# Chunked attention and two MLPs on one core: later issue of raw weight loads, g fetched three steps ahead, other places for late k, q, v loads and for y's copies

## Chip, core and metric

One core of one Trainium2 chip runs the whole program. The metric is device time in microseconds (us) of one execution, the median of several. Engines are named as in the profile: PE (matmul), PEld (its weight load), DVE, ACT, POOL and SP. SP issues nearly all loads, POOL the stores to scratch tensors in DRAM.

## Reference

Attention runs inside chunks of 64 tokens, and its result goes through two MLPs:

```python
scores = scale * np.matmul(q_c, k_c.transpose(0, 1, 2, 4, 3))     # q, k, v: (4, 8, 576, 64), chunks of 64
attn = softmax(scores)
x = (attn @ v_c)  -> (2304 tokens, 512)
x = ((x @ w_a) * (x @ w_b)) @ w_out                               # d_ff 1536
h = x @ w_in                                                      # d_ff 2048
g = (a0 + a1*h + a2*h**2 + a3*h**3) / (1 + |b0|*|h| + |b1|*h**2 + 1e-6)
out = g @ w_out2
```

All inputs are read as pairs of 32-bit words where they are 64-bit numbers (the weights), and every product is made from a high and a low part of both factors: three matmuls for one.

## The kernel before

**The order of the program.** One core walks through five stages. (1) The head: attention of the first 768 tokens (units of 128 tokens, numbered `u`, 0 to 5), in an order written out by hand in two lists. `LOADS` is the order of the first loads on SP's queue; `FIRST` is the order of the work: `k0` transposes k of unit 0, `S` makes scores, `X` the exponential, `E` the softmax's division, `P` transposes the result, `V` multiplies with v, `L` makes the low part of x, `w` is one piece of a weight's conversion, and `d4` puts 4 matmuls on a constant tile with no use for their result on PE (`warm`). Units 0 to 2 are done in the head, 3 to 5 within the next stage. (2) `ab_half`: x times `w_a` and `w_b` for the first 768 tokens, with attention of the other tokens between. (3) `s_step`: the same products for the other tokens, in a scheme with seven products for eight. Both store g = a*b to DRAM, `g_d[i]` for the 12 blocks `i` of d_ff. (4) The y stage: 5 blocks of tokens `j` (256, then 512 each) by 12 blocks `i`, `y_part(j, i)`, which fetches g back from DRAM (`g_fetch`), splits it in high and low (`g_parts`, the cast on ACT at L650, the difference on DVE at L652), and adds into four PSUM tiles `acc[j][d]`. Those are copied out by `y_out` (ACT, L673) and stored by POOL. (5) `step2`: the second MLP.

**Weights.** A raw weight tile (512 KB, 64-bit) is loaded by `w_fetch` (L169), converted in four pieces (`w_piece`), and split into high and low. The pieces are spread through the program by `w_until`. Piece 0 reads the raw tile on ACT (L214) and DVE (L218), piece 2 reads it for the last time on ACT (L223). The first 24 tiles (`w_a`, `w_b` alternating, named w_a_0, w_b_1, w_a_2, ... by their number) have 4 raw buffers, the later ones 2. Loads of the tiles behind are issued in pieces 0 and 2 by `w_fetch_ahead`. Each waits on SP until the buffer's last reader, L223 of the tile 4 or 2 before, is done, and all that stands behind it on SP's queue waits too.

**Small buffers.** Fetched g, fetched y, converted tiles `w_x`, g to be stored and copies `ys` share six buffers (`p_io`, tag `io`). `g_hi` and `g_lo` have two each.

**Order between engines.** The schedule is manual: every engine runs its instructions in the order in which the code calls them. In the y stage a step `n` issues `g_fetch` of step n+2, then `g_parts` of step n+1, pieces of weights, then `y_part` of step n, and `evacuate(1)` takes one `y_out` from the list `evac`. In step2's first calls the list is emptied after the front of the second MLP. PSUM tile `ps_ab` "a" holds `acc[4][2]` in the last block and is then the tile of the third `h_part` (L247 to L249, h).

Of the kernel before, what the change touches and what calls it, by code (L numbers as in the profile page):

```python
# [20 lines left out]
def chunk_attention_two_mlps(  # L21
# [34 lines left out]
    nc = tc.nc  # L56
    P = 128
# [7 lines left out]
    KD = DM // P  # L65
    F1 = DFF1 // P
# [11 lines left out]


    FIRST = (  # L80
        "k0 d2 q0 k1 q1 S0 X0 d4 S1 X1 k2 E0 w w q2 E1 P0 S2 w w V0 d2 P1 X2 L0 w w V1 E2 w w L1 d2 P2 w w V2 L2 w"
    ).split()
    LOADS = "k0 q0 k1 q1 w v0 k2 q2 w v1 v2 w k3 q3 w k4 q4 v3 k5 q5 v4 v5".split()

    AHEAD = 4
    NWP = 12 - AHEAD
# [54 lines left out]
    order1 = [(n, i) for i in range(F1) for n in ("a", "b")]  # L141
# [41 lines left out]
    def w_fetch_ahead(n):  # L183
        while n_cv[0] < n_cv[2] and n_cv[0] < n + (AHEAD if n_cv[0] < len(order1) else 2):
            w_fetch()

    def w_hi(n):
        if n in f32s:
            key = order[n]
            wt[key] = w_tile(key, F32R)  # L190
            nc.scalar.copy(wt[key][0], f32s[n].bitcast(F32))

    def w_lo(n):
        if n in f32s:
            hi, lo = wt[order[n]]
            nc.vector.tensor_tensor(lo, f32s.pop(n).bitcast(F32), hi.bitcast(F32), ALU.subtract)

    def w_piece():


        n, piece = divmod(n_cv[1], 4)
        n_cv[1] += 1
        key = order[n]
        if piece == 0:
            w_fetch_ahead(n)
            t = raws.pop(key)

            terms[n] = (t, *w_tile(key, I32))
        t, c, z = terms[n]
        hw = t[:, :, 1]  # L210
        lw = t.rearrange("p f t -> p (f t)").bitcast(U16).rearrange("p (f t) -> p f t", t=4)[:, :, 1]
        zz = z.bitcast(F16).rearrange("p (f t) -> p f t", t=2)
        if piece == 0:
            nc.scalar.activation(zz[:, :, 1], hw.bitcast(F32), AF.Copy, scale=2.0 ** -112)  # L214
            if 8 <= n < len(order1) + len(ordero):
                nc.scalar.activation(c.bitcast(F32), hw.bitcast(F32), AF.Copy, scale=2.0 ** -112)
            else:
                nc.vector.tensor_scalar(c.bitcast(F32), hw.bitcast(F32), 2.0 ** -112, None, ALU.mult)  # L218
        elif piece == 1:
            w_hi(n - 1)  # L220
            nc.vector.tensor_scalar(c, c, 3, None, ALU.logical_shift_left)
        elif piece == 2:
            nc.scalar.activation(zz[:, :, 0].bitcast(U16), lw, AF.Copy, scale=2.0 ** -13)  # L223
            w_lo(n - 1)
            w_fetch_ahead(n + 1)
        else:
            del terms[n]
            x = f32s[n] = p_io.tile([P, DM], I32, name="w_x", tag="io")
            nc.vector.tensor_tensor(x, c, z, ALU.add)
            if key in w1_d:  # L230
                nc.gpsimd.dma_start(out=w1_d[key], in_=x.bitcast(F32))

    def w_until(tiles):

        while n_cv[1] < min(4 * tiles, 4 * n_cv[2]):
            w_piece()
# [14 lines left out]
    def cols(pair, k):  # L251
        return [t[:, k * P:(k + 1) * P] for t in pair]
# [43 lines left out]
    def a_load(u, *names):  # L296

        (b0, c0), (b1, c1) = divmod(2 * u, NCH), divmod(2 * u + 1, NCH)
        for nm, src in (("k", k), ("q", q), ("v", v)):
            if nm not in names or u >= NU:  # L300
                continue
            if u < 2 * UH:
                if ("raw", u) not in un:
                    un["raw", u] = p_X.tile([P, 3, H, D], F32, name="kqv", tag=f"X{NQ - 1}_{u + 1}")
                t = un["raw", u][:, "kqv".index(nm)]
            else:
                t = p_qk.tile([P, H, D], F32, name=nm, tag=nm, bufs=2 if nm == "v" else 1)
            if b0 == b1:
                parts = [(t, src[b0, :, c0 * CH:(c0 + 2) * CH, :])]
            else:  # L310
                parts = [
                    (t[c * CH:(c + 1) * CH], src[bb, :, cc * CH:(cc + 1) * CH, :])
                    for c, (bb, cc) in enumerate(((b0, c0), (b1, c1)))
                ]
            for dst, s in parts:
                nc.sync.dma_start(out=dst, in_=s.rearrange("h s d -> s h d"))  # L316
            raw[nm, u] = t
# [154 lines left out]
    ca_t = const.tile([P, 4], F32, name="ca_t")  # L472
    cb_t = const.tile([P, 2], F32, name="cb_t")
# [156 lines left out]
    acc = {}  # L630
    evac = []
# [9 lines left out]
    def g_fetch(j, i):  # L641
        t = p_io.tile([P, SIZES[j]], F32, name="g_raw", tag="io")
        nc.sync.dma_start(out=t, in_=g_d[i][:, START[j]:START[j] + SIZES[j]])
        raw["g", j, i] = t
# [9 lines left out]
    def y_part(j, i):  # L654

        if i == 0:
            places = [(ps_acc, "acc")] * 2
            places += [(ps_at, "at")] * 2 if j % 2 else [(ps_ab, "a"), (ps_ab, "b")]
            acc[j] = [pool.tile([P, SIZES[j]], F32, name="acc", tag=tag) for pool, tag in places]
        w, (gh, gl) = wt["o", i], g1.pop((j, i))  # L660
        for d in range(KD):
            wh, wl = cols(w, d)
            nc.tensor.matmul(acc[j][d], wh, gh, start=i == 0, stop=False)  # L663
            nc.tensor.matmul(acc[j][d], wl, gh, start=False, stop=False)  # L664
        for d in range(KD):
            wh, wl = cols(w, d)
            nc.tensor.matmul(acc[j][d], wh, gl, start=False, stop=i == F1 - 1)  # L667
            if i == F1 - 1:
                evac.append(lambda d=d: y_out(j, d))

    def y_out(j, d):
        ys = p_io.tile([P, SIZES[j]], F32, name="ys", tag="io")
        nc.scalar.copy(ys, acc[j][d])  # L673
        nc.gpsimd.dma_start(out=y_d[:, d, START[j]:START[j] + SIZES[j]], in_=ys)

    def evacuate(n):
        for _ in range(min(n, len(evac))):
            evac.pop(0)()
# [122 lines left out]

    for item in LOADS:
        if item == "w":
            w_fetch()
        else:
            a_load(int(item[1]), item[0])
    nc.sync.dma_start(out=ca_t, in_=ca.unsqueeze(0).to_broadcast([P, 4]))
    nc.sync.dma_start(out=cb_t, in_=cb.unsqueeze(0).to_broadcast([P, 2]))
    nc.vector.memset(nlsh[:, 0:1], (1.0 + 1e-6) * 2.0 ** -LSH)
    nc.vector.memset(nlsh[:, 1:2], -LSH * math.log(2.0))  # L810

    for item in FIRST:
        if item == "w":
            w_piece()
            continue
        if item[0] == "d":
            warm(int(item[1:]))
            continue
        what, u = item[:-1], int(item[-1])
        if what in "kq":  # L820
            a_transpose(u, what)
        else:
            {"S": a_scores, "X": a_exp, "E": a_soft, "P": a_ptrans, "V": a_pv, "L": lambda u: un.pop(("lo", u))()}[
                what
            ](u)
    for u in (2 * UH, 2 * UH + 1):
        a_load(u, "k", "q", "v") if u == 2 * UH else a_load(u, "v")

# [35 lines left out]
    def half():  # L864


        n = n_half[0]
        n_half[0] += 1
        w_until(min(11 + 2 * n, 32) / 4 if n < 17 else (n + 18) / 4)
        if n_cv[1] == 32 or n_cv[1] == 4 * len(order1):  # L870
            w_flush()
        tick(0.5)
# [50 lines left out]
    w_until(n_cv[2])  # L923
    g_parts(0, 0)()
    g_fetch(0, 2)
    third, last = prev
    third()
    w_flush()
# [12 lines left out]
    places = [(j, i) for j in range(NB) for i in range(F1)]  # L941
# [2 lines left out]
    done = n_cv[1]  # L944
    a_ring = None
    for n, (j, i) in enumerate(places):
        if 0 < n < len(places) - 2:
            g_fetch(*places[n + 2])
        due = done + (4 * len(order2) * spent[n] // spent[-1] if n < len(spent) else 4 * len(order2))
        due -= n_cv[1]  # L950
        low = lambda: None
        if n + 1 < len(places):
            low = g_parts(*places[n + 1])
        if due:
            w_piece()
        low()
        for _ in range(due - 1):
            w_piece()
        if n:
            y_part(j, i)  # L960
        evacuate(1)
        if j == NB - 1:
            if 2 <= i < 2 + KD:
                y_split(0, i - 2)
            if 1 <= i < 1 + KD:
                y_fetch(0, i - 1)
            if i >= F1 - EARLY:
# [38 lines left out]
```

## Time and profile before

| | us |
|---|---|
| median of 3 runs (947.08 to 947.53) | 947.42 |
| the profiled execution's own time | 946.14 |
| span shown by its profile | 944.4 |
| PE busy within the span | 901.9 |

The profile is of one execution, whose time is 1.28 us below the median. The span is the stretch from the first to the last instruction, and the 1.74 us to the execution's time lie around it. An engine's busy time is of instructions alone; waits and the issuing of loads are not in it. PE is busy for 95% of the span, so what PE does not use is 42.5 us in all. PEclk is the share of full clock that PE was granted: 1.00 is 2.4 GHz and 0.50 is 1.2 GHz.

### The profile page before, as it was taken

What the parts mean: (1) busy time and instruction counts of PE and PEld (TensorE: products, weight loads), DVE (VectorE), ACT (ScalarE), POOL (GpSimd) and SP (SyncE); (2) the same over time, 40 slices, a digit from 0 to 9 for tenths busy, and PEclk for the clock granted to TensorE, in tenths of its full rate; (3) what the DMA queues carried; (4) which work ended last, traced back from release to release, by engine and by line L of the source; (5) the groups of instructions that cost most, each with busy time, mean ns of one, the idle gap of its engine ahead of it and who ended that gap; (6) DMA issues with size and microseconds to landing.
All of it is one profiled execution on the core that took longest, in us unless ns stands there. A gap on an engine that the chain in (4) does not pass through costs nothing.

```text
span 944.4 us, 14722 instructions
## 1 busy us (share of the span) xinstructions
PE 901.9 (95%) x5516; PEld 793.1 (84%) x5516; DVE 725.4 (77%) x1328; ACT 607.0 (64%) x1098; POOL 64.3 (7%) x122
## 2 busy tenths in 40 slices
PE   6879999999999999799998989999999999999998
PEld 5769998989999998676766889888888888888997
DVE  5657878588788875566656589899888988998886
ACT  5647887455555453466656478786777777776775
POOL 0111111111111111000000000000000000000000
PEclk9879999999999999999999999999999999999999
DMA  9957896333443413566776320020002002000100
GB/s 233 249 170 213 245 236 184 119 120 129 140 140 122 144 65 129 190 207 228 230 234 224 130 67 1 1 78 0 1 1 89 1 0 79 1 1 1 45 1 33
DMA packets 107335, 105.82 MB, mean 112 GB/s; under 512 B 61440, under 2 KB 84480, under 8 KB 107264
## 3 DMA queue, kind: packets, MB, share of 16 engines
q1 hardware_dynamic: 99264, 79.71, 29.1%
q0 software_dynamic: 8000, 25.17, 7.3%
q8 instruction: 43, 0.70, 0.3%
q14 instruction: 28, 0.23, 0.1%
HBM read 74.98 MB, written 29.88 MB: 111 GB/s over the span
## 4 chain that ended last, share of the span: by engine, by line
PE 52%; issue 24%; DMA 7%; ACT 5%; DVE 4%; SPq 4%; POOL 3%; POOLq 0%; ACTq 0%; DVEq 0%
PE h L247 7%; PE h L249 7%; PE acc L248 7%; PE h L248 7%; PE acc L247 7%; PE acc L249 7%; DMA g_raw<-g_d 6%; POOL g_d L487 3%; SPq L316 2%; PE ab L247 2%; PE ab L249 2%; PE ab L248 2%; ACT g_hi L650 1%; SPq L169 1%; PE acc L663 1%
## 5 line engine op out<-in xcount | busy, mean ns | idle before, releaser
L247 PE MATMUL h<-y,w_i 128*128 128x512 f32 (+1 forms) x320 | 118.7, 371 | 3.0 <-ACT ys L673 3.0
L249 PE MATMUL h<-y,w_i 128*128 128x512 f32 (+1 forms) x320 | 118.5, 370 | 0.0
L248 PE MATMUL h<-y,w_i 128*128 128x512 f32 (+1 forms) x320 | 118.3, 370 | 0.0
L724 ACT ACTIVATE a_ring<-h 128x512 f32<-128x512 f32 (+1 forms) x80 | 44.3, 554 | 99.6 <-PE h L249 99.5
L663 PE MATMUL acc<-g_hi,w_o 128*128 128x512 f32 (+1 forms) x240 | 90.2, 383 | 14.1 <-ACT g_hi L650 12.4
L573 ACT COPY s<-y 128x384 f32<-128x384 f32 x72 | 34.4, 479 | 84.6 <-PE y L249 83.0
L664 PE MATMUL acc<-g_hi,w_o 128*128 128x512 f32 (+1 forms) x240 | 87.9, 373 | 0.0
L727 DVE SCALAR_TENSOR_TENSOR u<-u,cb_t,a_ring 128x512 f32<-128x512 f32 (+1 forms) x80 | 55.7, 696 | 35.3 <-ACT u L725 34.4
L652 DVE TENSOR_TENSOR g_lo<-g_raw,g_hi 128x512 fp32r<-128x512 f32 (+1 forms) x60 | 38.1, 636 | 54.4 <-ACT g_hi L650 51.2
L248 PE MATMUL acc<-w_o,g_hi 128*128 128x512 f32 x191 | 75.3, 394 | 0.0
L650 ACT CAST g_hi<-g_raw 128x512 fp32r<-128x512 f32 (+1 forms) x60 | 34.1, 570 | 63.4 <-DMA g_raw<-g_d 49.0
L247 PE MATMUL acc<-w_o,g_hi 128*128 128x512 f32 x191 | 74.9, 392 | 0.0
L249 PE MATMUL acc<-w_o,g_lo 128*128 128x512 f32 x191 | 74.2, 389 | 0.0
L663 PEld LDWEIGHTS acc<-g_hi,w_o 128*128 128x128 f32 x240 | 45.3, 189 | 30.5 <-ACT g_hi L650 20.9
L247 PEld LDWEIGHTS h<-y,w_i 128*128 128x128 f32 x320 | 60.5, 189 | 12.2 <-ACT ys L673 3.3
L248 PEld LDWEIGHTS h<-y,w_i 128*128 128x128 f32 x320 | 60.6, 190 | 8.7
L249 PEld LDWEIGHTS h<-y,w_i 128*128 128x128 f32 x320 | 60.5, 189 | 7.5
L667 PE MATMUL acc<-g_lo,w_o 128*128 128x512 f32 (+1 forms) x240 | 60.9, 376 | 0.6 <-DVE g_lo L652 0.6
L726 ACT ACTIVATE t<-h,ca_t 128x512 f32<-128x512 f32 (+1 forms) x80 | 59.1, 738 | 0.0
L729 DVE SCALAR_TENSOR_TENSOR t<-t,ca_t,h 128x512 f32<-128x512 f32 (+1 forms) x80 | 55.6, 695 | 2.8
L737 DVE SCALAR_TENSOR_TENSOR u<-u,r 128x512 f32<-128x512 f32 (+1 forms) x80 | 50.5, 631 | 9.1 <-ACT r L736 9.1
L736 ACT ACTIVATE r<-r,nlsh 128x512 f32<-128x512 f32 (+1 forms) x80 | 54.6, 682 | 2.6
(196 smaller groups left out, 2444.0 us busy)
## 6 DMA issues: line engine op xcount, KB each, us to landing
w_raw<-in_moe_w_out_dram SPq DMA_DIRECT2D x28, 512.0 KB, 3.7
g_d<-g POOLq DMA_DIRECT2D x72, 192.0 KB, 2.4
g_raw<-g_d SPq DMA_DIRECT2D x48, 256.0 KB, 4.2
w_raw<-in_moe_w_in_dram SPq DMA_DIRECT2D x16, 512.0 KB, 3.9
w_raw<-in_moe_w_a_dram SPq DMA_DIRECT2D x12, 512.0 KB, 5.3
w_raw<-in_moe_w_b_dram SPq DMA_DIRECT2D x12, 512.0 KB, 5.3
out_dram<-o SPq DMA_DIRECT2D x18, 256.0 KB, 2.3
y_d<-ys POOLq DMA_DIRECT2D x16, 256.0 KB, 4.5
```

What stands on the lines that cost most here:

```text
L247: nc.tensor.matmul(ps, wh, xh, start=first, stop=False, **kw)
L248: nc.tensor.matmul(ps, wh, xl, start=False, stop=False, **kw)
L249: nc.tensor.matmul(ps, wl, xh, start=False, stop=last, **kw)
L663: nc.tensor.matmul(acc[j][d], wh, gh, start=i == 0, stop=False)
L664: nc.tensor.matmul(acc[j][d], wl, gh, start=False, stop=False)
L667: nc.tensor.matmul(acc[j][d], wh, gl, start=False, stop=i == F1 - 1)
L724: nc.scalar.activation(ah, ps, AF.Abs)
L726: nc.scalar.activation(t, ps, AF.Identity, scale=ca_t[:, 3:4], bias=ca_t[:, 2:3])
L727: nc.vector.scalar_tensor_tensor(u, u, cb_t[:, 0:1], ah, ALU.add, ALU.mult)
L729: nc.vector.scalar_tensor_tensor(t, t, ca_t[:, 1:2], ps, ALU.add, ALU.mult)
L736: nc.scalar.activation(r, r, AF.Exp, scale=-1.0, bias=nlsh[:, 1:2])
L737: nc.vector.scalar_tensor_tensor(u, u, 1.0 + 1e-6, r, ALU.add, ALU.mult)
```

## The change

Eight edits, none of which changes what is computed. The head gets 12 more `warm` matmuls. Loads of k5, q5, v3, v4 and v5 are taken from `LOADS` and stand in `FIRST` (the `+` items), so that three raw weight tiles come ahead of them; the two small constants `ca_t`, `cb_t` are loaded after the head's list. In the `ab_half` stage `w_until` is called for two pieces more. From the 24th tile on, `w_fetch_ahead` moves from piece 2 to piece 3. `g_fetch` runs three steps ahead. The first `y_part` puts three low matmuls ahead of the fourth d. And `y_out` takes d in the order 2, 3, 0, 1.

```diff
     FIRST = (
-        "... E1 P0 S2 w w V0 d2 P1 X2 L0 w w V1 E2 w w L1 d2 P2 w w V2 L2 w"
+        "... E1 P0 S2 w +k5 +q5 w V0 d2 P1 X2 L0 w w V1 d4 E2 w +v3 +v4 +v5 w "
+        "L1 d2 P2 d4 w w V2 d4 L2 w"
     ).split()
-    LOADS = "k0 q0 k1 q1 w v0 k2 q2 w v1 v2 w k3 q3 w k4 q4 v3 k5 q5 v4 v5".split()
+    LOADS = "k0 q0 k1 q1 w v0 k2 q2 w v1 v2 w k3 q3 w k4 q4".split()
...
         elif piece == 2:
             nc.scalar.activation(zz[:, :, 0].bitcast(U16), lw, AF.Copy, scale=2.0 ** -13)
             w_lo(n - 1)
+            if n < len(order1):
+                w_fetch_ahead(n + 1)
+        else:
             w_fetch_ahead(n + 1)
-        else:
             del terms[n]
...
-        for d in range(KD):
-            wh, wl = cols(w, d)
-            nc.tensor.matmul(acc[j][d], wh, gl, start=False, stop=i == F1 - 1)
-            if i == F1 - 1:
-                evac.append(lambda d=d: y_out(j, d))
+            if (j, i) == (0, 0) and d == KD - 2:
+                for x in range(d + 1):
+                    nc.tensor.matmul(acc[j][x], cols(w, x)[0], gl, start=False, stop=False)
+        for d in range(KD - 1 if (j, i) == (0, 0) else 0, KD):
+            nc.tensor.matmul(acc[j][d], cols(w, d)[0], gl, start=False, stop=last)
+        if last:
+            evac.extend(lambda d=d: y_out(j, d) for d in (2, 3, 0, 1))
...
-        w_until(min(11 + 2 * n, 32) / 4 if n < 17 else (n + 18) / 4)
+        w_until(min(13 + 2 * n, 32) / 4 if n < 17 else (n + 18) / 4)
...
     g_fetch(0, 2)
+    g_fetch(0, 3)
...
-        if 0 < n < len(places) - 2:
-            g_fetch(*places[n + 2])
+        if 0 < n < len(places) - 3:
+            g_fetch(*places[n + 3])
```

**SP's queue in the head.** These are the loads that follow v1 and v2. `kqv` is a unit's k, q or v, `w_raw` a raw weight tile, in the order w_a_2, w_b_3, then w_a_4, w_b_5, w_a_6. Before:

```order
L316 DMA kqv<-in_q_dram 64x8x64 x2
L316 DMA kqv<-in_v_dram 128x8x64
L316 DMA kqv<-in_k_dram 128x8x64
L316 DMA kqv<-in_q_dram 128x8x64
L316 DMA kqv<-in_v_dram 64x8x64 x2
L316 DMA kqv<-in_v_dram 128x8x64
L807 DMA ca_t<-in_moe_a_dram 128x4
L808 DMA cb_t<-in_moe_b_dram 128x2
L169 DMA w_raw<-in_moe_w_a_dram 128x4x256
L169 DMA w_raw<-in_moe_w_b_dram 128x4x256
L169 DMA w_raw<-in_moe_w_a_dram 128x4x256
```

And of the change:

```order
L319 DMA kqv<-in_q_dram 64x8x64 x2
L170 DMA w_raw<-in_moe_w_a_dram 128x4x256
L319 DMA kqv<-in_k_dram 128x8x64
L319 DMA kqv<-in_q_dram 128x8x64
L170 DMA w_raw<-in_moe_w_b_dram 128x4x256
L319 DMA kqv<-in_v_dram 128x8x64
L319 DMA kqv<-in_v_dram 64x8x64 x2
L319 DMA kqv<-in_v_dram 128x8x64
L170 DMA w_raw<-in_moe_w_a_dram 128x4x256
L834 DMA ca_t<-in_moe_a_dram 128x4
L835 DMA cb_t<-in_moe_b_dram 128x2
```

w_a_4 moves ahead of k5 and q5, w_b_5 ahead of v3 to v5, and w_a_6 ahead of the constants. What stands behind these rows (k6 and q6, v6 and v7, then w_b_7) has the same loads ahead of it as before.

**SP's queue in the y stage's first block.** `g_raw` are fetches of g, `w_raw` the raw tiles of the second MLP's weights. Before:

```order
L169 DMA w_raw<-in_moe_w_in_dram 128x4x256
L169 DMA w_raw<-in_moe_w_out_dram 128x1024
L643 DMA g_raw<-g_d_82 128x256
L643 DMA g_raw<-g_d_83 128x256
L643 DMA g_raw<-g_d_84 128x256
L643 DMA g_raw<-g_d_85 128x256
L169 DMA w_raw<-in_moe_w_in_dram 128x4x256
L643 DMA g_raw<-g_d_86 128x256
L643 DMA g_raw<-g_d_87 128x256
L643 DMA g_raw<-g_d_88 128x256
```

And of the change:

```order
L646 DMA g_raw<-g_d_82 128x256
L170 DMA w_raw<-in_moe_w_in_dram 128x4x256
L170 DMA w_raw<-in_moe_w_out_dram 128x1024
L646 DMA g_raw<-g_d_83 128x256
L646 DMA g_raw<-g_d_84 128x256
L646 DMA g_raw<-g_d_85 128x256
L646 DMA g_raw<-g_d_86 128x256
L646 DMA g_raw<-g_d_87 128x256
L170 DMA w_raw<-in_moe_w_in_dram 128x4x256
L646 DMA g_raw<-g_d_88 128x256
```

The numbers 82 to 88 are the blocks i = 3 to 9. The fetches of i = 7 and i = 8 now stand ahead of the third raw tile, which in both programs waits on SP for a piece on ACT. The last four fetches of the stage stand together at its end, as before.

**ACT at the end of the y stage.** `acc_5805` to `acc_5808` are before's four tiles `acc[4][0]` to `acc[4][3]`; in the change they are `acc_5822` to `acc_5825`. `h` is the second MLP's first product in its first and second step. Before:

```order
L673 COPY ys_6122<-acc_5805 128x512
L735 ACTIVATE r_6138<-u_6102,nlsh_144 128x384
L736 ACTIVATE r_6138<-r_6138,nlsh_144 128x384
L724 ACTIVATE a_ring_6088<-h_6125 128x384
L725 ACTIVATE u_6102<-h_6125,cb_t_143 128x384
L726 ACTIVATE t_6103<-h_6125,ca_t_142 128x384
L116 CAST g_hi_6150<-t_6103 128x384
L673 COPY ys_6154<-acc_5806 128x512
L673 COPY ys_6157<-acc_5807 128x512
L673 COPY ys_6160<-acc_5808 128x512
```

And of the change:

```order
L680 COPY ys_6137<-acc_5824 128x512
L742 ACTIVATE r_6153<-u_6117,nlsh_144 128x384
L743 ACTIVATE r_6153<-r_6153,nlsh_144 128x384
L731 ACTIVATE a_ring_6103<-h_6140 128x384
L732 ACTIVATE u_6117<-h_6140,cb_t_143 128x384
L733 ACTIVATE t_6118<-h_6140,ca_t_142 128x384
L117 CAST g_hi_6165<-t_6118 128x384
L680 COPY ys_6169<-acc_5825 128x512
L680 COPY ys_6172<-acc_5822 128x512
L680 COPY ys_6175<-acc_5823 128x512
```

The copy of d = 2, the tile that the third step of h takes over, moves from third to first place, ahead of the second step's work on ACT.

## Rows read from the trace of the kernel before

**Rows 1.** Stretches of all engines: start:end, length, busy (instructions), PEclk, DMA share, GB/s

```profile
20.00:40.00 20.00, 15.79 (x161) 14.16 (x162) 10.63 (x24) 11.92 (x24) 2.77 (x5) 0.74 1.01 245
40.00:60.00 20.00, 13.47 (x149) 11.06 (x147) 17.86 (x42) 12.26 (x23) 3.54 (x6) 0.91 0.88 260
60.00:80.00 20.00, 19.58 (x213) 18.22 (x214) 8.66 (x22) 9.92 (x20) 1.62 (x3) 0.83 0.36 102
80.00:360.00 280.00, 277.36 (x2235) 267.87 (x2234) 218.42 (x436) 166.41 (x320) 42.09 (x78) 1.00 0.51 153
360.00:560.00 200.00, 182.23 (x845) 147.67 (x844) 123.48 (x232) 117.21 (x211) 13.29 (x25) 0.98 0.58 192
560.00:920.00 360.00, 360.00 (x1648) 305.60 (x1647) 320.78 (x520) 266.01 (x461) 0.00 (x0) 1.00 0.06 20
```

**Rows 2.** PE's waits, 20 to 62 us: total us, times, longest

```profile
PE at L389 <- DVE x_lo L409: 3.2, 1, 3.2
PE at L372 <- DVE e L364: 2.6, 1, 2.6
PE at L325 <- ACT qT L327: 1.5, 1, 1.5
```

**Rows 3.** SP's issues in the head, in time: start us, us, what

```profile
22.14 1.10 SPq L316 DMA_DIRECT2D kqv<-in_v_dram  x1
...
31.52 0.38 SPq L169 DMA_DIRECT2D w_raw<-in_moe_w_a_dram  x1
...
42.91 0.96 SPq L169 DMA_DIRECT2D w_raw<-in_moe_w_b_dram  x1
```

**Rows 4.** ACT in the head, in time, with the wait before

```profile
37.83 0.78 ACT L214 ACTIVATE w_a<-w_raw 128x512 f16<-128x512 f32 x1 [3.12 <-DMA w_raw<-in_moe_w_a_dram]
...
51.49 0.81 ACT L214 ACTIVATE w_b<-w_raw 128x512 f16<-128x512 f32 x1
```

**Rows 5.** Landing of raw tiles, 0 to 70 us

```profile
DMA to landing us min/median/max: 3.8/6.3/8.3
```

**Rows 6.** Matmuls of `warm` on PE, in time (two records a matmul)

```profile
9.35 1.16 PE L799 MATMUL at<-ident 128*128 128x128 f32 x8
17.48 1.22 PE L799 MATMUL at<-ident 128*128 128x128 f32 x4
```

**Rows 7.** PE's waits, 365 to 560 us

```profile
PE acc L663 <- ACT g_hi L650: 12.4, 15, 2.2
PE h L247 <- ACT ys L673: 3.0, 1, 3.0
PE acc L663 <- DVE g L616: 1.6, 1, 1.6
```

**Rows 8.** One late fetch of g in the first block: ACT, SP and PE, each in time

```profile
376.74 0.79 ACT L223 ACTIVATE w_i<-w_raw 128x512 uint16<-128x512 uint16 x1
...
381.68 0.40 ACT L650 CAST g_hi<-g_raw 128x256 fp32r<-128x256 f32 x1 [3.21 <-DMA g_raw<-g_d]
...
377.55 0.38 SPq L169 DMA_DIRECT2D w_raw<-in_moe_w_in_dram  x1
377.99 1.45 SPq L643 DMA_DIRECT2D g_raw<-g_d  x3
...
376.58 0.62 PE L667 MATMUL acc<-g_lo,w_o 128*128 128x256 f32 x4
377.94 0.62 PE L667 MATMUL acc<-g_lo,w_o 128*128 128x256 f32 x4
...
382.14 0.39 PE L663 MATMUL acc<-g_hi,w_o 128*128 128x256 f32 x1 [2.23 <-ACT g_hi L650]
```

**Rows 9.** Landing of fetched g, 365 to 560 us

```profile
DMA to landing us min/median/max: 2.0/4.1/6.0
```

**Rows 10.** ACT's copies of the last block of y, in time

```profile
541.67 0.59 ACT L673 COPY ys<-acc 128x512 f32<-128x512 f32 x1 [0.57 <-PE acc L667]
...
546.28 1.58 ACT L673 COPY ys<-acc 128x512 f32<-128x512 f32 x3
```

More of the change, by code (lines that the diff above doesn't have):

```diff
@@ L80, in chunk_attention_two_mlps @@
     FIRST = (
-        "k0 d2 q0 k1 q1 S0 X0 d4 S1 X1 k2 E0 w w q2 E1 P0 S2 w w V0 d2 P1 X2 L0 w w V1 E2 w w L1 d2 P2 w w V2 L2 w"
+        "k0 d2 q0 k1 q1 S0 X0 d4 S1 X1 k2 E0 w w q2 E1 P0 S2 w +k5 +q5 w V0 d2 P1 X2 L0 w w V1 d4 E2 w +v3 +v4 +v5 w "
+        "L1 d2 P2 d4 w w V2 d4 L2 w"
     ).split()
-    LOADS = "k0 q0 k1 q1 w v0 k2 q2 w v1 v2 w k3 q3 w k4 q4 v3 k5 q5 v4 v5".split()
+    LOADS = "k0 q0 k1 q1 w v0 k2 q2 w v1 v2 w k3 q3 w k4 q4".split()
     AHEAD = 4
@@ L660, in y_part @@
         w, (gh, gl) = wt["o", i], g1.pop((j, i))
+        last = i == F1 - 1
         for d in range(KD):
@@ L806, in chunk_attention_two_mlps @@
             a_load(int(item[1]), item[0])
-    nc.sync.dma_start(out=ca_t, in_=ca.unsqueeze(0).to_broadcast([P, 4]))
-    nc.sync.dma_start(out=cb_t, in_=cb.unsqueeze(0).to_broadcast([P, 2]))
     nc.vector.memset(nlsh[:, 0:1], (1.0 + 1e-6) * 2.0 ** -LSH)
@@ L818, in chunk_attention_two_mlps @@
             continue
+        if item[0] == "+":
+            a_load(int(item[2]), item[1])
+            continue
         what, u = item[:-1], int(item[-1])
@@ L825, in chunk_attention_two_mlps @@
             ](u)
+    nc.sync.dma_start(out=ca_t, in_=ca.unsqueeze(0).to_broadcast([P, 4]))
+    nc.sync.dma_start(out=cb_t, in_=cb.unsqueeze(0).to_broadcast([P, 2]))
     for u in (2 * UH, 2 * UH + 1):
```

## Prediction

> **What bounds the kernel now.** I first read the stretches of all engines [rows 1]. From 80 to 360 us and from 560 to 920 us PE is busy all the time (277.36 of 280, 360.00 of 360) at full clock: nothing that reorders loads can give time there. Two places are left. The head, 20 to 80 us, has 4.21, 6.53 and 0.42 us without PE work, and its mean clock is 0.74, 0.91 and 0.83. A clock of 0.50 for x of 20 us makes a mean of 1 - x/40, so the low level held for 10.4, 3.6 and 6.8 us; work done there would have taken half, so up to 5.2, 1.8 and 3.4 us are lost besides. The y stage, 360 to 560 us, has 17.8 us without PE work, and its 0.98 means about 8 us at the low level, up to 4 us lost. Both places together hold 11.2 + 10.4 + 17.8 + 4 = 43 us; that is the ceiling.
>
> Then the waits. In the head PE waits for DVE (x_lo 3.2, softmax 2.6) and for a copy on ACT (qT 1.5) [rows 2]. Behind DVE stands ACT, which waits 3.12 us at 37.83 for raw tile w_a_4 [rows 4], whose load SP issued only at 31.52, though it had reached v3, the load ahead of k5, by 22.14 [rows 3]. DMA is full there (share 1.01 at 245 GB/s) and DVE nearly so from 40 on (17.86 of 20) [rows 1]. In the y stage 12.4 of the 17.8 us are PE waiting for the cast of g_hi, in 15 pieces, 3.0 for one copy ys, and 1.6 for a g product [rows 7].
>
> The fetch that makes PE late is seen once in full [rows 8]. ACT runs L223 at 376.74 (0.79 us), SP can issue the raw tile behind it only at 377.55, three fetches of g stand behind that and go out from 377.99, the cast finds its g at 381.68 after a wait of 3.21, and PE starts at 382.14 after 2.23. So it is not bandwidth (share 0.58 in the stage [rows 1]) but order: a load of g stands on SP behind a load that waits for ACT, and ACT then waits for that g.
>
> **The change part by part.**
>
> *g three steps ahead, raw loads a piece later.* A fetch lands after 4.1 us, at most 6.0 [rows 9]. A step of the first block takes 1.36 us (377.94 - 376.58 [rows 8]), so two steps are 2.7 us and three 4.1. What counts is when SP is free: today the fetch that follows a blocked raw load is wanted by ACT two steps after the L223 that frees it. In the change the raw load stands a piece later, a step after its L223 in this block, so it meets a buffer that is already free, and the fetch behind it is one step further ahead: about four steps, 5.4 us, against 4.1. In the long blocks steps are twice as long, and the margin doubles. The raw tiles lose a piece of lead, but keep five pieces, more than two long steps, against a landing of at most 8.3 in the full DMA of the head [rows 5] and less in this stage; nothing waits. What is late next are the six small buffers: three fetches live at once instead of two leave fewer free ones, above all while ys and y copies pass (three blocks' ends). Of 12.4 I take 10; below, 3 (only the first block cured), above all 12.4.
>
> *Clock and restarts there.* With the waits the falls of the clock should go: 4 at most [rows 1], I take 2.5, below 0.
>
> *y's copies.* The first copy of the last block is done by 542.3, the others start at 546.28 [rows 10], as ACT has the second step's work between. PE's 3.0 us wait [rows 7] is for d = 2, third in the row. As first one it is ready before PE asks, so all 3.0 go; below, if only the place among the last three counted, two copies of 0.53 (1.58/3), 1.1.
>
> *First y_part.* Three low matmuls fill part of the 1.6 us wait: 12 matmuls of a step take 1.36, so three take 0.34. I take 0.3.
>
> *Raw tiles earlier in the head.* w_a_4 now goes out some 9 us earlier (22.14 against 31.52). ACT's 3.12 us wait goes, and with it DVE's chain up to x_lo. The next late thing is w_b_7: its load has the same bytes ahead of it as before, in a full DMA, so it still goes out near 42.9 and lands 6.3 later [rows 3, 5], at 49.2; ACT reads it at 51.49 now [rows 4]. So at least 2.3 us are gained; at most the three waits of [rows 2], 7.3. The program is better ordered behind w_b_7 (two pieces more are done ahead of it), so I take the middle, 5. What this moves back is hidden: k5 and q5 go behind one raw tile (512 KB at 245 GB/s, 2.1 us), v3 to v5 behind two; the longest waits of PE in this stretch [rows 2] are for DVE and ACT, and the one at q is for ACT's copy, not for a load. Without that cover k5 and q5 would cost up to 2.1 us.
>
> *Twelve warm matmuls.* Four cost 1.16 us at full clock, two up to 1.22 at the low one [rows 6]: 12 are 3.5 to 7.3 us, put where PE has 4.21 us of idle time in 20 to 40. At full clock they fit and cost nothing; at the low one they push the first x w_a product back by up to 3. In exchange the first dense matmuls may run at full clock: of 10.4 us lost at the low level in 20 to 80 I take 3 net, between -3 and +10.4.
>
> Here a page bears. The row shows the mean clock at 0.74 in 20 to 40 [rows 1], after a stretch in which PE kept stopping. The Trainium skill ("TensorE: Matmul & The Clock Gate", "Part 1: The HAM clock gate") says that the throttled clock is the default and that sustained activity releases it; by that rule the fill alone would win the whole 5.2 us of 20 to 40, where my 3 covers all three stretches, and the time would come out 2.2 us lower. The trace agrees as to the direction; how much activity suffices no row says, and I keep 3.
>
> *Two pieces more, constants later.* The pieces fill DVE's time in a stretch where it is 43% busy (8.66 of 20 in 60 to 80); the constants are first used in later stages. Nothing.
>
> **Sum.** 5 + 3 + 10 + 2.5 + 3 + 0.3 = 23.8 us. From the profiled execution's own 946.14: 922.3. The median of the runs is 1.28 above that execution, and I forecast a median: **923.6 us**. With all terms at their best (7.3 + 10.4 + 12.4 + 4 + 3 + 0.3 = 37.4) it would be 910.0, at their worst (2.3 - 3 + 3 + 0 + 1.1 + 0.3 = 3.7) 943.7.
>
> **Rivals.** *A: the head gives nothing.* The DMA is full and DVE is at 17.86 of 20 [rows 1], so w_a_4 earlier only makes w_b_7, or the warm matmuls, the wait. For it: same bytes, same DMA. Against: DVE idles while ACT waits for w_a_4. Then 15.8 of the y stage are left: 931.6.
>
> *B: the fetches stay late.* The six buffers fill, SP waits for ys stores instead of for L223. For it: POOL's stores hold buffers for microseconds at each block's end. Against: 15 waits are spread over all blocks. Only 3 of the 10 and none of the clock: 23.8 - 9.5 = 14.3, so 933.1.
>
> *C: slower.* The same six buffers, but in every step: a fetch three ahead takes the buffer that DVE frees in the step before, and the raw load behind it then comes too late for L214 on ACT, which is in order, so casts and copies stall too. With the head and ys as forecast (5 + 3 + 3 + 0.3 = 11.3), the stage's waits must grow from 12.4 past 23.7, that is 0.5 us in each of the 48 long steps, before the kernel is slower. At 0.75 a step, 36 us of waits: 947.4 - 11.3 + 23.6 = 959.7. Against it: the release is on DVE, which has time there (123.48 of 200 [rows 1]).
>
> A page gives a rule for a smaller loss of this kind. The Trainium skill ("DMA: Bandwidth & Descriptors", "Queues, rings and completion order") says that each DMA engine consumes a queue's descriptors in ring order. By that rule k5 to v5 come 2.1 to 4.2 us later, as reckoned above from 245 GB/s, and would lengthen the head if PE had been waiting for them; it had not [rows 2], so I leave the sum. Its chance is within A.
>
> *D: no effect.* Waits only move to the next late load: 946 to 948.
>
> **How the numbers follow.** Chances: forecast 0.58, A 0.17, B 0.16, C 0.04, D 0.05. The forecast's own range, with 2 us on each side for the head's terms and 4 for the stage's, is 917 to 930. For 8 in 10 the range reaches to A and B, 931.6 and 933.1, and below to where the clock term and the waits both come out well: 914 to 935. Within 0.2%, 1.9 us of 947.42, is what a measurement of this kernel can't tell from no change. Faster: forecast, A, B, and a share of D: 0.92; same 0.03; slower 0.05.
>
> **What would show it.** Right: SP issues w_a_4 near 22 us; ACT's wait at L214 is gone; PE's wait for x_lo ends some 5 us earlier and is shorter; PEclk in 20 to 40 is above 0.8. In the y stage PE's wait for g_hi falls from 12.4 to about 2, SP's waits for L223 nearly vanish, the wait for ys is gone, and the stage is about 15 us shorter. The stretches at 80 to 360 and 560 to 920 keep their lengths. Wrong: a new ACT wait for w_b_7 as long as w_a_4's was; SP waits for ys stores or DVE of the length that L223's had; a low clock that persists to 32 us after the warm matmuls.

## The result and the profile after

| kernel | median, us | runs | ratio to before, 95% interval |
|---|---|---|---|
| before | 947.25 | 943.76 to 947.53 | |
| the change | 921.06 | 918.80 to 922.81 | 0.973 [0.9699, 0.9762] |

The change is 26 us faster. Its profiled execution took 920.83 us, span 919.1. The forecast of 923.6 and its range held, and the measured median lies 2.5 us below the forecast.

Where the time came from is read by laying the two traces beside each other at points that both programs pass: the first product of the y stage, the first product h of the second MLP (the stretches are cut 0.1 us ahead of it), and that MLP's first product into `acc`. First the start of the y stage, PE in time, in before:

```profile
366.34 0.28 PE L663 MATMUL acc<-g_hi,w_o 128*128 128x256 f32 x1
```

and after:

```profile
359.27 0.28 PE L667 MATMUL acc<-g_hi,w_o 128*128 128x256 f32 x1
```

So all that lies before this point gave 7.1 us. Now the two stretches that follow, up to the first h and from there to the first product into `acc` of the second MLP (columns as in [rows 1]). Before:

```profile
366.34:537.20 170.86, 156.08 (x715) 123.19 (x715) 105.66 (x199) 100.34 (x177) 10.40 (x19) 0.99 0.62 206
537.20:553.30 16.10, 13.11 (x63) 12.20 (x62) 8.31 (x15) 9.84 (x20) 2.15 (x4) 0.89 0.31 108
```

After:

```profile
359.27:516.60 157.33, 152.20 (x715) 125.80 (x715) 105.90 (x199) 103.12 (x177) 10.49 (x19) 0.98 0.70 227
516.60:527.80 11.20, 11.20 (x62) 10.62 (x61) 5.46 (x10) 7.16 (x14) 0.54 (x1) 1.00 0.29 91
```

The products of y are 13.5 us shorter with the same 715 instructions: 9.7 us less without work (14.8 to 5.1), and 3.9 us less in the work itself, as a matmul behind a stop takes longer (shown below). The seam to the second MLP is 4.9 us shorter: 3.0 of idle time, and 1.9 of work that ran at a clock of 0.89 and now runs at 1.00. Only the first of these belongs to the change for certain (see the copies of y below). Behind the seam both have the same left: 944.4 - 553.3 = 391.1 and 919.1 - 527.8 = 391.3. The sum, 7.1 + 13.5 + 4.9 - 0.2 = 25.3, is the difference of the spans.

The stretches that answer to [rows 1]:

```profile
20.00:40.00 20.00, 17.30 (x223) 15.26 (x221) 16.01 (x36) 14.39 (x28) 2.85 (x6) 1.00 1.08 276
40.00:60.00 20.00, 14.12 (x163) 12.19 (x159) 14.04 (x33) 10.38 (x21) 2.88 (x5) 0.91 0.90 257
60.00:80.00 20.00, 19.81 (x229) 17.89 (x228) 12.15 (x28) 13.24 (x26) 2.71 (x5) 1.00 0.69 186
80.00:360.00 280.00, 277.01 (x2179) 268.70 (x2178) 216.68 (x432) 162.44 (x314) 42.01 (x78) 1.00 0.49 147
```

In 20 to 40 DVE and ACT do more (16.01 against 10.63, 14.39 against 11.92): weights are converted earlier. From 80 to 360 PE is as busy as before (277.01 against 277.36). SP's issues of raw tiles in the head, after, to [rows 3]:

```profile
22.84 1.44 SPq L170 DMA_DIRECT2D w_raw<-in_moe_w_a_dram  x1
...
26.73 2.41 SPq L170 DMA_DIRECT2D w_raw<-in_moe_w_b_dram  x1
...
42.67 1.55 SPq L170 DMA_DIRECT2D w_raw<-in_moe_w_b_dram  x1
```

and ACT's reads of those tiles, to [rows 4]:

```profile
30.07 0.79 ACT L215 ACTIVATE w_a<-w_raw 128x512 f16<-128x512 f32 x1
...
41.62 0.79 ACT L215 ACTIVATE w_a<-w_raw 128x512 f16<-128x512 f32 x1 [3.27 <-DMA w_raw<-in_moe_w_a_dram]
...
49.36 0.79 ACT L215 ACTIVATE w_b<-w_raw 128x512 f16<-128x512 f32 x1 [3.56 <-DMA w_raw<-in_moe_w_b_dram]
```

w_a_4 goes out at 22.84 instead of 31.52, ACT reads it at 30.07 (the first row) instead of 37.83, and the wait for it is gone. Now ACT waits for w_a_6 (3.27) and for w_b_7 (3.56). w_b_7 still goes out behind the same bytes (42.67 against 42.91). w_a_6 goes out later than before (33.57 against 32.55), though the constants no longer stand ahead of it: w_b_5 took SP 2.41 us to issue, and v3 to v5 behind it 4.27.

PE in time shows where the head's 7.1 us arise. The rows are the product with v (`pT,kqv`) that waits for x_lo in before, and the transpose of q that comes one product with v later. Before:

```profile
60.42 1.38 PE L389 MATMUL at<-pT,kqv 64*64 64x64 f32 x32 [3.16 <-DVE x_lo L409]
...
65.76 1.11 PE L325 MATMUL at<-ident,q 128*128 128x128 f32 x4
```

After:

```profile
55.37 1.01 PE L392 MATMUL at<-pT,kqv 64*64 64x64 f32 x32 [1.60 <-issue]
...
58.57 0.65 PE L328 MATMUL at<-ident,q 128*128 128x128 f32 x4
```

The product with v starts 5.1 us sooner and the transpose of q 7.2. So 2.1 us are gained between the two, by the clock: in before a matmul of `ab` takes 0.52 us there (62.96), after it 0.33 (56.98). PE's waits from 335 to 560 us, after, to [rows 7]:

```profile
PE acc L673 <- DVE g_lo L655: 3.8, 1, 3.8
PE acc L667 <- ACT g_hi L653: 0.8, 1, 0.8
PE acc L667 <- DVE g L619: 0.5, 1, 0.5
```

The 12.4 us for g_hi are 0.8, the 3.0 for ys are gone, and one wait has grown, that for g_lo, from 0.6 us in before to 3.8:

```profile
PE acc L667 <- DVE g_lo L652: 0.6, 1, 0.6
```

Behind the 3.8 is DVE, which waits for a store of g (DVE in time; L626 computes the last tile of g, which `s_step` stores):

```profile
365.97 0.56 DVE L626 TENSOR_TENSOR g<-q,s 128x384 f32<-128x384 f32 x1 [3.72 <-DMA g_d<-g]
```

That tile takes one of the six small buffers, and a fetch of g more is under way than before.

### The profile page after: what moved, and what is told of

Same layout as the page of the kernel before. It is cut to its first block, busy times and chain, and to the rows that moved or that the text cites. A ratio compares the mean times of both kernels' runs of the same rounds, so it can differ in the third digit from the quotient of the medians.

```text
span 919.1 us, 14781 instructions
## 1 busy us (share of the span) xinstructions
PE 890.8 (97%) x5540; PEld 789.3 (86%) x5540; DVE 725.0 (79%) x1328; ACT 610.0 (66%) x1098; POOL 64.4 (7%) x122
## 4 chain that ended last, share of the span: by engine, by line
PE 60%; issue 30%; POOL 5%; DMA 2%; DVE 2%; ACT 1%; POOLq 0%; SPq 0%; DVEq 0%
PE acc L251 7%; PE h L252 7%; PE h L250 7%; PE acc L250 7%; PE h L251 7%; PE acc L252 7%; PE acc L673 5%; PE acc L668 5%; PE acc L667 5%; POOL g_d L490 4%; DMA y_raw<-y_d 1%; DMA g_d<-g 1%; POOL w_b L234 1%; POOL w_a L234 1%; PE at L328 1%
## 5 line engine op out<-in xcount | busy, mean ns | idle before, releaser
L655 DVE TENSOR_TENSOR g_lo<-g_raw,g_hi 128x512 fp32r<-128x512 f32 (+1 forms) x60 | 38.2, 638 | 32.5 <-ACT g_hi L653 18.2
L742 ACT ACTIVATE r<-u,nlsh 128x512 f32<-128x512 f32 (+1 forms) x80 | 55.6, 694 | 0.3
```

The costliest lines, as they stand in the source:

```text
L742: nc.scalar.activation(r, u, AF.Ln, scale=2.0 ** -LSH, bias=nlsh[:, 0:1])
```

## Experiments

Twelve kernels, each the change with one edit undone or one load moved (`e_best2` with two), or before with a part of the change. Times of before moved between 940.87 and 949.85 in the sessions, so a ratio is good to about 0.3%, 3 us. Where effects are smaller, two numbers of each profile help: the time of the first y product (all that the head does to the time), and the rest of the span behind it. Seven profiles whose heads are the same (the change, `e_head_only`, `e_g3_behind`, `e_piece2`, `e_two_ahead`, `e_y_order`, `e_g3_last`) have the first product at 358.25 to 361.72: a move of less than 3 us there means little from one profile. Six profiles whose y stages are the same (the change, `e_y_only`, `e_no_warm`, `e_loads_back`, `e_b7_first`, `e_half_back`) have the rest at 559.2 to 560.9: there a move of 2 us counts. With before's y stage and its many stops the rest varies more, 574.4 in `e_head_only` against 578.1.

| kernel | median, us | ratio, 95% interval | first y product | rest of the span |
|---|---|---|---|---|
| before | 947.25 | | 366.34 | 578.1 |
| the change | 921.06 | 0.973 [0.9699, 0.9762] | 359.27 | 559.8 |
| e_head_only | 938.34 | 0.9938 [0.9914, 0.9962] | 360.83 | 574.4 |
| e_y_only | 928.52 | 0.9814 [0.9771, 0.9858] | 366.39 | 560.9 |
| e_no_warm | 920.30 | 0.9731 [0.9695, 0.9767] | 359.14 | 559.2 |
| e_g3_behind | 921.17 | 0.9745 [0.9704, 0.9785] | 361.72 | 561.3 |
| e_piece2 | 924.13 | 0.9779 [0.9747, 0.981] | 359.65 | 563.8 |
| e_two_ahead | 919.01 | 0.9726 [0.9694, 0.9759] | 358.32 | 558.4 |
| e_y_order | 924.08 | 0.978 [0.9747, 0.9813] | 358.25 | 562.4 |
| e_loads_back | 929.43 | 0.9837 [0.9802, 0.9871] | 365.90 | 560.2 |
| e_g3_last | 916.51 | 0.9705 [0.9676, 0.9733] | 358.53 | 557.6 |
| e_b7_first | 919.81 | 0.9735 [0.9707, 0.9764] | 356.50 | 559.8 |
| e_half_back | 921.50 | 0.9756 [0.9728, 0.9785] | 359.98 | 560.2 |
| e_best2 | 915.16 | 0.9697 [0.9668, 0.9726] | 357.66 | 555.2 |

**The head's edits alone, and the rest alone.** `e_head_only` is before with the two lists, the constants' place and the two pieces more; `e_y_only` is before with the other four edits.

> The kernel before with the head's edits alone (order of the loads, twelve warm matmuls, two pieces more, late constants); the y stage as before. Theory: the gains of head and y stage are separate and add, so this has the head's alone, 7 to 8 us: 939 to 941 against 947.3, and PE starts the first y product about 7 us earlier than before, with a y stage of before's length. Rival: the y stage's waits depend on when the head's loads end, or most of the gain needs both: then under 3 us, or over 12.

> The kernel before with the y stage's edits alone (raw loads a piece later, g three steps ahead, first y product, order of the copies); the head as before. Theory: 17 to 19 us faster, 928 to 931, with the wait for g_lo of 3.8 us at the stage's start in it too. Rival (not separate): under 14 us.

The head alone moves the first product by 5.5 us, a little less than the 7 expected, and the y stage then has its old waits, as PE's rows there show:

```profile
PE acc L665 <- ACT g_hi L651: 12.1, 13, 1.9
PE h L248 <- ACT ys L675: 3.0, 1, 3.0
```

The rest is still 3.7 us shorter than in before, which was not expected. The waits don't explain it; the mean clock of the execution does in part (0.994 against 0.984), and 1.6 of the 3.7 lie in the seam, as shown below.

The y stage's edits alone leave the first product where it was and shorten the rest by 17.2. The two ratios multiplied, 0.9938 x 0.9814 = 0.9753, lie within the interval of the change: the parts add.

**What in the head does it.** Three kernels, each the change with one of the head's edits undone.

```diff
 # e_loads_back
-    ... S2 w +k5 +q5 w V0 d2 P1 X2 L0 w w V1 d4 E2 w +v3 +v4 +v5 w ...
+    ... S2 w w V0 d2 P1 X2 L0 w w V1 d4 E2 w w ...
-    LOADS = "... k4 q4"
+    LOADS = "... k4 q4 v3 k5 q5 v4 v5"        (ca_t, cb_t behind it, as before)
 # e_no_warm
-    ... V1 d4 E2 ... P2 d4 w w V2 d4 L2 w
+    ... V1 E2 ... P2 w w V2 L2 w
 # e_half_back
-        w_until(min(13 + 2 * n, 32) / 4 if n < 17 else (n + 18) / 4)
+        w_until(min(11 + 2 * n, 32) / 4 if n < 17 else (n + 18) / 4)
```

> The kernel of the change with the loads of the head in the order of before (k5, q5, v3, v4, v5 and the two small constants ahead of the raw tile for w_a_4); the twelve extra warm matmuls, the pace of the pieces and all else stay. Theory (the head's 6 to 7.6 us come from the earlier raw tiles): ACT waits some 3 us for w_a_4 again, the first S product starts 5 to 7 us later than in the change, and the time is 5 to 7 us above it. Rival (the head's gain is the pace of the pieces, or comes from the y stage): the time is within 2 us of the change's.

> The changed kernel without the twelve warm matmuls; loads stay moved. Theory: the warm matmuls keep PE's clock at its upper level from 20 to 32 us, so without them the clock there falls to 0.50 as before and 2 to 4 us are lost: 923 to 925 against the change's 921. Rival 1: the earlier raw tiles alone keep PE busy enough, the clock stays at 1.00 and the time is the same or up to 1 us better, as the matmuls cost room. Rival 2: later waits for raw tiles w_a_6 and w_b_7 take up the loss, and V of unit 4 starts at 55 us all the same: within 1 us, at a low clock.

> The kernel of the change with the pace of the weight's pieces in the products of a and b as before (11 + 2n instead of 13 + 2n). Theory (the pace is worth nothing by itself, PE is busy from 80 us on either way; the head's gain is the order of the loads): within 1.5 us of the change. Rival (the two pieces more are what lets the raw tiles be asked for in time in the head): ACT waits for raw tiles 2 us longer in all between 40 and 62 us, and the time is 2 to 4 us above the change's.

With the loads in the old order the first y product is at 365.90, as in before, though warm matmuls and pace are those of the change; the ratio's interval lies wholly above that of the change. The medians are 8.4 us apart, the two profiled spans 7.0; expected were 5 to 7. So the order of SP's queue is what the head's gain needs: without it the warm matmuls and the pace give 0.4 us (365.90 against 366.34). The new order without these two was not run. ACT's row for w_a_4 in `e_loads_back`:

```profile
37.99 0.78 ACT L214 ACTIVATE w_a<-w_raw 128x512 f16<-128x512 f32 x1 [7.14 <-DMA w_raw<-in_moe_w_a_dram]
```

It is read at 37.99, in before at 37.83 [rows 4], but the wait is 7.14 instead of 3.12: ACT was through with what stands ahead of it 3.9 us sooner (30.85 against 34.71), and only waited longer for the same tile. In part that is the pace: it puts this read ahead of two copies (a qT and a kT) that stand ahead of it in before, and PE then waits 6.6 us for that qT, where its longest wait for a qT in before was 1.5 [rows 2].

Without the twelve warm matmuls the time doesn't change (the second rival came, not the theory). The clock does, as the stretches of `e_no_warm` show (0.83 where the change has 1.00, then 1.00 where it has 0.91):

```profile
20.00:40.00 20.00, 16.59 (x200) 14.65 (x201) 14.38 (x34) 15.32 (x30) 3.59 (x6) 0.83 1.08 257
40.00:60.00 20.00, 13.76 (x191) 11.72 (x190) 16.17 (x39) 11.15 (x23) 2.69 (x5) 1.00 0.94 274
```

but w_b_7 is read at nearly the same time as in the change (49.36), after a shorter wait, and the product with v of the rows above then starts at 55.79, in the change at 55.37:

```profile
49.78 0.80 ACT L215 ACTIVATE w_b<-w_raw 128x512 f16<-128x512 f32 x1 [3.21 <-DMA w_raw<-in_moe_w_b_dram]
```

The pace of the pieces is not told from nothing: 359.98 lies within the spread of the same head, and the interval overlaps that of the change.

**Which edit cures the waits for g.** Each of the two undone by itself.

```diff
 # e_piece2: a raw tile behind the 24th is issued in piece 2 again
-            if n < len(order1):
-                w_fetch_ahead(n + 1)
-        else:
             w_fetch_ahead(n + 1)
+        else:
             del terms[n]
...
 # e_two_ahead: g two steps ahead again
     g_fetch(0, 2)
-    g_fetch(0, 3)
...
-        if 0 < n < len(places) - 3:
-            g_fetch(*places[n + 3])
+        if 0 < n < len(places) - 2:
+            g_fetch(*places[n + 2])
```

> The kernel of the change with one edit undone: a raw tile is issued at piece 2 again, g stays three steps ahead. Theory (the fetches of g stood on SP behind a raw tile that waited for its slot; the later issue removes that wait, and the extra step of lead is only margin): the raw tiles wait on SP again (SP's waits for w_o and w_i rise by some 10 us or more in the last stretch), but with three steps of lead PE still finds most of g; PE's waits for g_hi stay under 5 us and the time is within 6 us of the change's. Rival (the later issue does it all): g_hi waits come back to 10 to 12 us, and the time is 8 to 13 us above the change's.

> The kernel of the change with the other edit undone: g two steps ahead, a raw tile still a piece later. Theory (either edit is nearly enough by itself): g_hi waits of 2 to 5 us, the time within 5 us of the change's; the wait of DVE for the last tile of g (3.7 us) goes too, since there is one tile less in flight, which may even give 2 us back. Rival (the lead does it all): g_hi waits of 10 to 12 us, the time 8 to 13 us above the change's.

PE's waits in the y stage of `e_piece2`:

```profile
PE acc L671 <- DVE g_lo L653: 4.4, 1, 4.4
PE acc L665 <- ACT g_hi L651: 3.1, 5, 0.8
```

and of `e_two_ahead`:

```profile
PE acc L667 <- ACT g_hi L653: 3.0, 5, 1.3
PE acc L667 <- DVE g L619: 1.0, 1, 1.0
PE acc L673 <- DVE g_lo L655: 0.6, 1, 0.6
```

Either edit by itself leaves 3 of the 12.4 us, both together 0.8: the first of them does the work, whichever it is. They differ in their price. With g two steps ahead the wait for g_lo is 0.6 instead of 3.8, and the stage is not longer than in the change (558.4 against 559.8). So the third step of lead, as the change makes it, gains 2.2 us of g_hi and gives 3.2 back. With the raw tile at piece 2 the rest is 3.9 us longer. SP's waits for the last readers of w_o and w_i rise by some 6 us there, not by the 10 expected.

**The copies of y.**

```diff
-            evac.extend(lambda d=d: y_out(j, d) for d in (2, 3, 0, 1))
+            evac.extend(lambda d=d: y_out(j, d) for d in range(KD))
```

> The kernel of the change with the copies of y in the order 0, 1, 2, 3 again. Theory (the next chunk's first product waits for the buffer that is copied last): PE waits about 3 us in one place for ys, and the clock after it costs up to 1.7 us more: the time is 3 to 5 us above the change's. Rival (with g at hand the wait is hidden or moves to the next product): under 1 us, no difference.

The wait is back, 3.0 us in one place, and the rest of the span is 2.5 us longer (the intervals of the ratios overlap):

```profile
PE h L250 <- ACT ys L680: 3.0, 1, 3.0
```

The seam from the first h to the first product into `acc` of the second MLP is 14.4 us long here, 3.3 longer than in the change (11.1), at full clock:

```profile
514.92:529.35 14.43, 11.45 (x62) 10.59 (x61) 8.12 (x15) 9.64 (x20) 2.15 (x4) 1.00 0.23 80
```

`e_head_only`, with the same wait of 3.0 us, has 14.4 us and 1.00 too. Of the three profiles with that wait only the one of before shows a fallen clock behind it (0.89), and there the seam took 16.0. So the edit is worth 3.3 us of the seam; the other 1.6 are the clock of one execution.

**The new wait for g_lo.** If the fourth fetch holds the buffer that the last tile of g needs, putting it later should cure it. `e_g3_behind` puts it behind the end of the products of g, `e_g3_last` also behind the first raw tiles of the second MLP.

```diff
     g_fetch(0, 2)
-    g_fetch(0, 3)
...
     y_part(0, 0)
     last()
+    g_fetch(0, 3)             (e_g3_behind)
...
     w_fetch_ahead(len(order1) + len(ordero))
+    g_fetch(0, 3)             (e_g3_last)
```

> The changed kernel with the fetch of g's fourth block moved behind the last product of the stage before, so that it doesn't take one of the six small buffers ahead of the last g tile. Theory: DVE's wait of 3.7 us for a store, at the last g, comes from that buffer; it goes, and with it PE's wait of 3.8 us for g_lo and the low clock behind it (6.9 us at 0.50, 3.4 lost): 914 to 917. Rival: the store itself is late (the loads beside it fill the DMA), and the wait stays at 2 us or more: 919 to 921; or the fourth fetch is now late and PE waits at the third or fourth step for 2 us or more.

> The kernel of the change with the fetch of g's fourth tile moved behind the first raw tiles of the second MLP on SP's queue; everything else of g stays three steps ahead. Theory (in the change that fetch takes the buffer that the last tile of g needs, and DVE and then PE stand 3.7 and 3.8 us for it; put behind the raw tiles it delays neither): DVE's wait and PE's wait for g_lo fall under 1.5 us each, PE's waits for g_hi stay under 3, and the time is 2 to 4 us below the change's, near that of the kernel with g two steps ahead (919.0). Rival (some tile waits in any case, only another): one wait of 3 us or more for g_lo or g_hi remains near 365 to 375 us, and no difference.

In `e_g3_behind` DVE no longer waits for a store at L626, but nothing is gained, where 4 to 7 us were expected. SP in time (the first row is four fetches and their waits, the second the first raw tile of the second MLP):

```profile
346.84 18.09 SPq L646 DMA_DIRECT2D g_raw<-g_d  x4
364.98 1.00 SPq L170 DMA_DIRECT2D w_raw<-in_moe_w_in_dram  x1
```

The fourth fetch waits for a buffer on SP, and the raw tile behind it goes out at 364.98, in the change at 359.38. ACT then waits for that tile, and PE again for g_lo (3.7 us in two places). ACT's row:

```profile
372.07 0.78 ACT L215 ACTIVATE w_i<-w_raw 128x512 f16<-128x512 f32 x1 [4.48 <-DMA w_raw<-in_moe_w_in_dram]
```

With the raw tiles ahead of the fetch (`e_g3_last`) SP's rows are

```profile
343.66 10.72 SPq L646 DMA_DIRECT2D g_raw<-g_d  x3
354.47 0.38 SPq L170 DMA_DIRECT2D w_raw<-in_moe_w_in_dram  x1
354.90 0.50 SPq L170 DMA_DIRECT2D w_raw<-in_moe_w_out_dram  x1
```

the raw tile goes out at 354.47, and PE's waits in the stage are

```profile
PE acc L667 <- DVE g L619: 2.2, 1, 2.2
PE acc L667 <- ACT g_hi L653: 0.7, 2, 0.4
```

No wait for g_lo is left; 1.7 us came back at L619, where DVE waits 1.6 us for a store of g. The rest of the span is 2.2 us shorter than in the change, and its four times (915.25 to 917.90) all lie below those of the change. So the wait did come from the buffers, and a fetch that waits must not stand ahead of a load that someone needs.

**The tile that the head waits for now.** `e_b7_first` issues k6, q6, v6 and v7 behind the raw tile for w_b_7; `e_best2` is this and `e_g3_last` together.

```diff
     for u in (2 * UH, 2 * UH + 1):
-        a_load(u, "k", "q", "v") if u == 2 * UH else a_load(u, "v")
+        todo.append((1.5, n_todo[0], lambda u=u: a_load(u, "k", "q", "v") if u == 2 * UH else a_load(u, "v")))
+        n_todo[0] += 1
```

> The kernel of the change with the raw tile for w_b_7 issued ahead of the loads of k6, q6, v6 and v7 (their issue moves behind it on SP's queue, nothing else). Theory (ACT's wait of 3.56 us for that tile is what the head waits for now): the tile is issued near 38 instead of 42.7, ACT's wait for it is under 1 us, the first S product starts 2 to 4 us earlier, and the time is 2 to 4 us below the change's. Rival (DMA's share is 1.08 and 0.90 there, so the tile lands no earlier, or PE then waits for the softmax on DVE instead): the first S product moves by less than 1 us and so does the time.

> Both of the first two edits together (g's fourth tile behind the raw tiles; the raw tile for w_b_7 ahead of k6, q6, v6, v7). Theory: their gains lie in different stages and add, 4 to 8 us below the change. Rival: only one of them gives something, 2 to 4 us.

In `e_b7_first` SP issues the tile at 36.67, not 42.67:

```profile
36.67 0.44 SPq L170 DMA_DIRECT2D w_raw<-in_moe_w_b_dram  x1
```

ACT reads it without a wait, 5.3 us sooner than in the change:

```profile
44.10 0.76 ACT L215 ACTIVATE w_b<-w_raw 128x512 f16<-128x512 f32 x1
```

but PE waits for the softmax on DVE as long as in the change, and only 1.6 us sooner. `e_b7_first`, then the change:

```profile
46.75 0.66 PE L375 MATMUL at<-ident,e 128*128 128x128 f32 x4 [2.76 <-DVE e L367]
...
48.35 1.12 PE L375 MATMUL at<-ident,e 128*128 128x128 f32 x4 [2.76 <-DVE e L367]
```

The first y product is at 356.50, and at 357.66 in `e_best2`, both ahead of the earliest of the seven profiles with the change's head (358.25). Their mean is 357.1, that of the seven 359.5: of 5.3 us about 2 come through. The medians (919.81 and 921.06) don't tell `e_b7_first` from the change. `e_best2` has the shortest rest of all, 555.2, no wait over 1.1 us in the y stage, and with 915.16 the lowest median here. Its rest is 4.6 us below the change's, more than the spread there, and its five times (914.65 to 917.09) lie below the four of the change, though the intervals of the ratios overlap. Its first product, 1.6 us earlier, says little by itself. Why its rest is 2.4 us below that of `e_g3_last` no run shows.

## Why the prediction was right, by its steps

**Raw tiles earlier in the head (5, between 2.3 and 7.3), warm matmuls (3, between -3 and 10.4).** Measured for all of the head: 7.1 (366.34 to 359.27). Nearly all of it needs the order of the loads: `e_loads_back` gives 6.6 of it back, `e_no_warm` nothing. So the first term was near its upper bound, and the second was 0; that their sum, 8, came close is luck. The step that failed is "the first dense matmuls may run at full clock: ... I take 3 net". The clock did rise, 1.00 against 0.83 without the twelve matmuls, but ACT's wait for w_b_7 took it up (3.56 us, 3.21 without them). The Trainium skill ("TensorE: Matmul & The Clock Gate", "Part 1: The HAM clock gate") says that sustained activity releases the throttled clock; the trace agrees (1.00 against 0.83), and by that rule alone the fill was to win 5.2 us. A faster PE gains nothing ahead of a tile that lands when it lands. Rival A's condition thus held for the warm matmuls, not for w_a_4.

That w_b_7 would be late next was right to a few tenths: issue forecast near 42.9, measured 42.67; landing forecast at 49.2, ACT's read at 49.36 after 3.56 us. The wait for that tile, as long as w_a_4's had been, was also one of the prediction's signs of being wrong; it came, and the time was right all the same. At ACT's read only 2.1 us are gained (51.49 to 49.36), as the lower bound said. The other 5 come behind it. DVE reads the tile 5.4 us sooner, as the two pieces of w_a_6 that ran ahead of that read (at 51.48 and 54.18 in before) are done by 48.90; before, then after:

```profile
54.78 0.42 DVE L218 TENSOR_SCALAR w_b<-w_raw 128x512 f32<-128x512 f32 x1
...
49.36 0.43 DVE L219 TENSOR_SCALAR w_b<-w_raw 128x512 f32<-128x512 f32 x1 [0.46 <-DMA w_raw<-in_moe_w_b_dram]
```

x_lo follows, and PE's product with v comes 5.1 us sooner, with half the idle time ahead of it (1.60 against 3.16). The last 2.1 us are the clock behind this shorter stop. So the clock did give something in the head, but at 60 us and not by the warm matmuls: in `e_no_warm` it is 1.00 from 60 to 80 too.

**g three steps ahead, raw loads later (10, between 3 and 12.4).** The wait for g_hi fell by 11.6. Two things in this step were wrong. SP's waits for the last reader of a raw buffer did not nearly vanish: for w_o they were 26.0 us after, for w_i 24.6,

```profile
SPq L170 <- ACT w_o L224: 26.0, 14, 3.0
SPq L170 <- ACT w_i L224: 24.6, 13, 4.3
```

where before had

```profile
SPq L169 <- ACT w_o L223: 33.6, 13, 4.5
SPq L169 <- ACT w_i L223: 26.1, 13, 4.1
```

(both 365 to 560 us; total, times, longest). SP waits nearly as long, but what stands behind it on the queue is no longer late. And the six buffers, named as late next but given no term of their own, cost 3.2 us in one place (the wait for g_lo, 0.6 to 3.8): at the last tile of g that `s_step` stores, not at the blocks' ends. Net the waits gave 8.4 us here, and the wait for g 1.1 more (1.6 to 0.5), for which the first `y_part` was given 0.3; that edit was not run by itself, so its part stays open.

**Clock and restarts (2.5, between 0 and 4).** Measured 3.9 in the work of the 715 instructions, though the clock of this stretch did not rise (0.99 and 0.98). What became shorter is the matmul behind each stop, which before shows:

```profile
401.43 0.50 PE L663 MATMUL acc<-g_hi,w_o 128*128 128x512 f32 x1 [0.81 <-ACT g_hi L650]
401.76 0.40 PE L664 MATMUL acc<-g_hi,w_o 128*128 128x512 f32 x1
402.00 0.40 PE L663 MATMUL acc<-g_hi,w_o 128*128 128x512 f32 x1
```

Behind a stop it takes 0.50 us and the next starts 0.33 later; in a dense row a matmul takes 0.40 and the next starts 0.24 later, inside it. So a stop lengthens the work by (0.40 - 0.24) + (0.33 - 0.24) = 0.25 us, and 14 stops fewer (17 to 3) make 3.5, an estimate from these rows. The term came out above 2.5, but from restarts and not from the clock.

**y's copies (3, between 1.1 and 3).** The wait of 3.0 went as reckoned, and `e_y_order` puts the edit at 3.3 us of the seam and 2.5 of span. The 4.9 us by which the seam is shorter hold 1.6 more, because its work ran at 0.89 of full clock in the one profiled execution of before; the same wait in two other kernels left it at 1.00.

**Sum.** Forecast 23.8, measured 25.3 in the spans: head 8 against 7.1, the rest 15.8 against 18.2. Rivals B, C and D did not come: the wait for a store that B and C reckoned with cost PE time once, not in every step. Without the 1.6 us of clock in the seam the measured sum would be 23.7.

## What to carry to other kernels

On one issuing queue a load that must wait for a buffer delays everything behind it. So order the queue by when the reader needs the data and when the buffer is free, and look first at which reader waits for which load, and what stood ahead of it. Either an earlier fetch or a later blocker was enough here; the second of the two cures took away 2 us more of waits, and more lead took a buffer that cost 3. When a late tile sets the pace, getting to it sooner doesn't count: w_a_4 was read at 37.8 and 38.0 us with waits of 3.1 and 7.1. And what an in-order engine then has behind the late read waits too (the qT above).

## What the runs showed of the hardware

The time that SP takes to issue a load varies widely. The raw tiles of `w_b` in the change, 512 KB each, took from 0.37 to 2.41 us to issue between 26.7 and 52.2 us (minimum, median, maximum in ns):

```profile
L170 SPq DMA_DIRECT2D w_raw<-in_moe_w_b_dram x4: 368/998/2414, 26.7 to 52.2; - x4
```

In the y stage such a tile took 0.38 to 0.50 (`e_g3_last` above). The long issues stand where the DMA share is 0.90 to 1.08, but a full DMA alone doesn't make them: before issues w_a_4 at 31.52 in 0.38 us [rows 3], at a share of 1.01. What does is not shown. So in the head a load put ahead of another can cost the queue this time too, and not only its bytes.

The clock does not always fall behind the same stop. At the end of the y stage PE waits 3.0 us in before, `e_head_only` and `e_y_order`; the work of the seam then ran at a mean clock of 0.89, 1.00 and 1.00, and the seam took 16.0, 14.4 and 14.4 us.
